# Issue queues by role, earlier X loads and later weight copies in the prologue of a spectral-filter and recurrent-attention kernel

## Chip, cores, metric

One core of one Trainium2 chip. The metric is the device time of one execution in microseconds (us); lower is better.

## The reference

Two independent computations share one launch, and their results are put side by side.

```python
# A: gated long convolution, q,k,v: (1, 2048, 1024)
kv  = k_shift(k, shift_k) * v               # 4-tap shift
y_f = rfft2(pad(kv)) * rfft2(pad(ssm_k))    # product in the frequency domain
y   = irfft2(y_f)[:2048] + kv * ssm_D
a   = q * y
# B: attention with a carried memory, x: (1, 2048, 1024), 32 heads of 128
for s in range(64):                         # 64 segments of 32 rows
    h = concat([mem, x[segment s]])         # mem: 8 rows
    qh, kh, vh = h @ Wq, h @ Wk, h @ Wv
    o = softmax(mask(qh @ kh.T * scale)) @ vh @ Wo
    mem = o[:8]                             # needed by the next segment
    b[segment s] = o[8:]
out = concat([a, b], axis=-1)
```

## The kernel before

The program has a prologue of about 460 us and a loop over the 64 segments of about 1736 us. The prologue computes A completely and, in between, those products of B that don't depend on the memory. It has these stages; I mark them by the instructions of TensorE (PE) and use these names throughout:

1. **Stage 1** (to the first matmul `kb_ps`): the first transform of A. The **first dense pass** follows (to the first `Kre_ps`): matmuls of B alone.
2. **Spectral stage** (to the last `z_ps`): 34 units, each of which gathers columns of two scratch tensors in HBM (`SK`, `SU`), multiplies in the frequency domain and stores to scratch `SZ`. After each unit `fill()` slips in a piece of B.
3. **Inverse stage** (to the last `y_ps`): 16 steps, each loads `zt` from `SZ` and `qt` from q, and writes one block of the output.
4. **Last dense pass** (to the first `vb_ps`), then the **V pass** (to the first `acc`, which is the start of the loop): x times Wv, stored to scratch `VBD`.

Each `nc.<engine>.dma_start` is an instruction in the in-order queue of that engine: while it waits for its source or its buffer, what is behind it in this queue isn't issued either. (In the profile before, SyncE's queue waits for an output's `ot` from 320.7 to 324.9 us; the `zt` load behind this output goes out right after it, at 325.3 us.) SyncE (SP in the profile) only issues; ScalarE (ACT) and GpSimd (POOL) compute and issue. The parts that matter, cut:

```python
# spectral stage
gather(Kt_, SK1, pr, nc.scalar)
gather(Ut, SU1, pr, nc.sync)
...
nc.gpsimd.tensor_tensor(out=Yre, in0=pa, in1=pb, op=ALU.subtract)
...
scatter(SZ, pr, zss[pi], nc.sync)           # waits for ScalarE's zs
# inverse stage
for t in range(16):
    (nc.sync if t % 2 == 0 else nc.gpsimd).dma_start(zt[:], SZ...[t])
    ...                                     # 4 matmuls into pt
    load_rows(qt, q, t, 0, nc.gpsimd if t % 2 == 0 else nc.sync)
    nc.vector.tensor_tensor(out=ot[:], in0=pt[:], in1=qt[:], op=ALU.mult)
    nc.sync.dma_start(rows_view(outa, t), ot[:])   # waits for VectorE's ot
    fill()
# pieces of B
def x_block(b):
    both = pair()                           # two buffers, taken in turn
    xq[b % 2].dma_start(both[:, 0:1024], x[...])   # xq = [nc.sync, nc.gpsimd]
    ...                                     # 8 transposes on PE, a copy on VectorE
    nc.gpsimd.dma_start(REC[...], xt)       # REC<-pair; frees the buffer
def fill():
    store()                                 # one waiting REC<-stage store, nc.gpsimd
    n = units[0]; units[0] += 1
    if n < 34 and n % 3 == 2 or n >= 34 and n % 3 == 0:
        if blocks: x_block(blocks.pop(0))
    if n >= 34 or n % 3 != 2:
        next(rest, None)                    # next head of a dense pass
# V pass
wv = [group(2, 0, temps), None]             # Wv loads on nc.sync
for _ in rest: store()                      # last dense pass
wv[1] = group(2, 1, temps)
place_late(4, stage_home); ...              # Wlate, Wmore loads, nc.gpsimd
for ch in ring_order:                       # copies HBM to HBM for the loop
    if ch[0] == 3:                          # the 6 streamed chunks of Wo
        nc.gpsimd.dma_start(dst_view(stream_src(ch), ch), dram_chunk(ch))
for g in range(2):
    for tb in range(4):
        vst = pair()...                     # the same two buffers
        for c in range(4):
            ...                             # 8 matmuls vb_ps, then evac to vst
        for c in range(4):
            nc.sync.dma_start(VBD[...], vst[:, c, :]...)
```

The Wo copies stand late in the source but wait for nothing, so the compiler's scheduler put them near the start of GpSimd's queue.

Of the kernel before, what the change touches and what calls it, by code (L numbers as in the profile page):

```python
# [31 lines left out]
def a_kernel(ctx: ExitStack, tc, q, k, v, shift_k, ssm_k, ssm_D, outa, slot4, slot16, stage1_done, fill):  # L32
    nc = tc.nc
# [18 lines left out]
    def rows_view(ap2d, t):  # L52
        return ap2d.rearrange("(p r) d -> r p d", r=16)[t]

    def load_rows(dst, src2d, t, lag, eng):
        c = t - lag
        if c >= 0:
            eng.dma_start(dst, rows_view(src2d, c))
        else:
            nc.gpsimd.memset(dst[0:1, :], 0.0)  # L60
            rv = rows_view(src2d, 16 + c)
            eng.dma_start(dst[1:113, :], rv[0:112])
            eng.dma_start(dst[113:128, :], rv[112:127])
# [205 lines left out]
    with ExitStack() as c2:  # L269
# [4 lines left out]
        def gather(dst, scratch, pr, eng):  # L274
            if pr <= 31:
                eng.dma_start(dst[:, :], scratch[4 * pr:4 * pr + 4].rearrange("m n d -> (m n) d"))
            else:
                eng.dma_start(dst[0:32, :], scratch[1])
                nc.gpsimd.memset(dst[32:64, :], 0.0)
                nc.gpsimd.memset(dst[64:128, :], 0.0)  # L280

        def scatter(scratch, pr, src, eng):
            if 1 <= pr <= 31:
                eng.dma_start(scratch[4 * pr:4 * pr + 4].rearrange("m n d -> (m n) d"), src[:, :])
            elif pr == 0:
                eng.dma_start(scratch[0], src[0:32, :])
                eng.dma_start(scratch[2:4].rearrange("m n d -> (m n) d"), src[64:128, :])
            else:
                eng.dma_start(scratch[1], src[0:32, :])

        def load_set(st):
            prs = [2 * st, 2 * st + 1] if st < 16 else [32]
            Us, Ks = [], []
            for pi, pr in enumerate(prs):
                Kt_ = gio.tile([128, 1024], BF, tag=f"Kg{pi}", name="Kg")
                gather(Kt_, SK1, pr, nc.scalar)
                Ut = gio.tile([128, 1024], BF, tag=f"Ug{pi}", name="Ug")
                gather(Ut, SU1, pr, nc.sync)
                Us.append(Ut)
                Ks.append(Kt_)  # L300
            return prs, Us, Ks
# [34 lines left out]
        def unit_back(st, prs, hf, Ys, zss):  # L336
            Yre, Yim = Ys
            for pi, pr in enumerate(prs):
                pt = ps1.tile([128, 512], F32, tag="p", name="z_ps")
                rs = slice(64 * pi, 64 * pi + 64)  # L340
                nc.tensor.matmul(pt[:, :], lhsT=Nre[rs, st, :], rhs=Yre[rs, :], start=True, stop=False,
                                 tile_position=(64 * pi, 0))
                nc.tensor.matmul(pt[:, :], lhsT=Nim[rs, st, :], rhs=Yim[rs, :], start=False, stop=True,
                                 tile_position=(64 * pi, 0))
                nc.scalar.copy(zss[pi][:, hf * 512:(hf + 1) * 512], pt[:])
            if hf == 1:
                for pi, pr in enumerate(prs):
                    scatter(SZ, pr, zss[pi], nc.sync)

        pending = None  # L350
        nxt = load_set(0)
# [13 lines left out]
    with ExitStack() as c3:  # L365
        io = c3.enter_context(tc.tile_pool(name="a3_io", bufs=4, side="right"))
        wk = c3.enter_context(tc.tile_pool(name="a3_wk", bufs=3, side="right"))
        ps_big = c3.enter_context(tc.tile_pool(name="a3_ps", bufs=3, space=PSUM))
        for t in range(16):
            pt = ps_big.tile([128, 1024], F32, tag="big", name="y_ps")  # L370
            zt = io.tile([128, 2, 1024], BF, tag="zt", name="zt")
            (nc.sync if t % 2 == 0 else nc.gpsimd).dma_start(zt[:], SZ.rearrange("m (h r) d -> r m h d", h=2)[t])
            for hf in range(2):
                for h in range(2):
                    nc.tensor.matmul(pt[:, hf * 512:(hf + 1) * 512], lhsT=G2h[h][:, :],
                                     rhs=zt[:, h, hf * 512:(hf + 1) * 512], start=(h == 0), stop=(h == 1))
            qt = io.tile([128, 1024], BF, tag="qt", name="qt")
            load_rows(qt, q, t, 0, nc.gpsimd if t % 2 == 0 else nc.sync)
            ot = wk.tile([128, 1024], BF, tag="ot", name="ot")
            nc.vector.tensor_tensor(out=ot[:], in0=pt[:], in1=qt[:], op=ALU.mult)  # L380
            nc.sync.dma_start(rows_view(outa, t), ot[:])
            fill()


def b_kernel(ctx: ExitStack, tc, x, mem0, Wq, Wk, Wv, Wo, outb, n_seg, run_a):
    nc = tc.nc
# [42 lines left out]
    def stream_src(ch):  # L429
        return WS[ring_order.index(ch), :, 0:2048]  # L430
# [87 lines left out]
    def make_xbt():  # L518
        xb = x.rearrange("(tb s t) d -> tb s t d", s=16, t=SEG)
        for tb in range(4):  # L520
# [5 lines left out]
            for h in range(2):  # L526
                nc.scalar.copy(XBT[h][:, :, 16 * tb:16 * tb + 16, :].rearrange("p k s t -> p k (s t)"),
                               tp[:, 512 * h:512 * h + 512].rearrange("p (k c) -> p k c", k=4))

    def group(m, g, temps={}, which=range(8), ws=None):  # L530
        ws = ws or [None] * 8
        for kc in which:
            ch = (m, kc, g)
            if ch in res:
                nc.sync.dma_start(res[ch], dram_chunk(ch))
                ws[kc] = res[ch]
            else:
                t = temps[ch]() if ch in temps else pw()
                nc.sync.dma_start(t[:], dram_chunk(ch))
                if ch in streamed:  # L540
                    nc.gpsimd.dma_start(stream_src(ch), t[:])
                ws[kc] = t[:]
        return ws

    def x_block(b):
        both = pair()
        X_sb = both[:, 0:1024]
        xq[b % 2].dma_start(X_sb, x[b * 128:(b + 1) * 128, :])
        tp = ps0.tile([128, 1024], BF, tag="ps0", name="xt_ps")
        for kc in range(8):  # L550
            nc.tensor.transpose(tp[:, kc * 128:(kc + 1) * 128], X_sb[:, kc * 128:(kc + 1) * 128], ident[:])
        xt = both[:, 1024:2048].rearrange("p (s k t) -> p s k t", s=4, k=8)
        nc.vector.tensor_copy(xt, tp[:].rearrange("p (k j t) -> p j k t", k=8, j=4))
        nc.gpsimd.dma_start(REC[:, 4 * b:4 * b + 4, 0:256], xt.rearrange("p s k t -> p s (k t)"))
# [51 lines left out]
    def fill():  # L606
        store()
        n = units[0]
        units[0] += 1
        if n < 34 and n % 3 == 2 or n >= 34 and n % 3 == 0:  # L610
            if blocks:
                x_block(blocks.pop(0))
        if n >= 34 or n % 3 != 2:
            next(rest, None)

    run_a(pw, slot16, stage1_done, fill)

# [42 lines left out]
    with c0p:  # L660
        temps = dict(zip(v_temp, homes_v))
        wv = [group(2, 0, temps), None]
        for _ in rest:
            store()
        wv[1] = group(2, 1, temps)
        while stores:
            store()
        place_late(4, stage_home)
        for i in range(len(v_temp) - 2, n_more):
            place_late(1, lambda: more(i))  # L670
        for _ in range(2):
            fetch()
        for ch in ring_order:
            if ch[0] == 3:
                nc.gpsimd.dma_start(dst_view(stream_src(ch), ch), dram_chunk(ch))
        for g in range(2):
            ws = wv[g]
            for tb in range(4):
                vst = pair()[:].rearrange("p (c w) -> p c w", c=4)
                for c in range(4):  # L680
                    ps = ps0.tile([128, 512], F32, tag="ps0", name="vb_ps")
                    for kc in range(8):
                        nc.tensor.matmul(ps[:], lhsT=xbt(kc)[:, 16 * tb:16 * tb + 16, :].rearrange("p s t -> p (s t)"),
                                         rhs=ws[kc][:, c * 512:(c + 1) * 512], start=(kc == 0), stop=(kc == 7))
                    evac(vst[:, c, :], ps[:])
                for c in range(4):
                    nc.sync.dma_start(
                        VBD[16 * tb:16 * tb + 16, :, c, :, g * 128:(g + 1) * 128].rearrange("s t i e -> (s t) i e"),
                        vst[:, c, :].rearrange("p (i e) -> p i e", i=4))
            if g == 0:  # L690
                place_late(4, stage_home)
                for i in range(2):
                    place_late(1, lambda: more(i))
        for i in range(2, len(v_temp) - 2):
            place_late(1, lambda: more(i))
        for k in (2, 3):
            if late:
                place_late(1, lambda: pw(k))
        assert not late
# [397 lines left out]
```

## Time and profile before

2196.51 us, median of 3 runs (2195.79 to 2200.39).

| what | number | view |
|---|---|---|
| loop, 64 segments | 1735.9 us, DMA share 1.00, 384 GB/s | windows |
| prologue | 459.7 us, of which the DMA engines idle some 50 to 60 us | windows |
| inverse stage | 74.9 us, DMA share 0.93 at 311 GB/s | windows |
| SyncE standing for `zs` and `ot` in the prologue | 42.3 and 40.2 us | waits |

The windows view of the kernel before: one row for each stage in the order above (the first dense pass is the second row, the loop the last). Columns as the second line says: busy us and number of instructions of each engine, granted TensorE clock, mean busy share of the 16 DMA engines, rate.

```profile
core 0: us, PE busy (x) PEld busy (x) DVE busy (x) ACT busy (x) POOL busy (x), PEclk, DMA share, GB/s
0.00:122.80 122.80, 69.02 (x297) 29.57 (x298) 101.17 (x205) 100.21 (x108) 33.77 (x55) 0.86 0.96 338
122.80:152.50 29.70, 29.70 (x130) 12.91 (x131) 3.46 (x5) 6.26 (x11) 0.00 (x0) 0.93 0.92 338
152.50:298.50 146.00, 125.92 (x683) 40.77 (x682) 109.20 (x189) 78.48 (x150) 66.61 (x68) 0.93 0.81 272
298.50:373.40 74.90, 49.46 (x212) 21.11 (x212) 24.62 (x25) 5.81 (x10) 22.48 (x32) 0.84 0.93 311
373.40:390.80 17.40, 17.40 (x82) 7.90 (x81) 4.47 (x9) 3.52 (x6) 1.81 (x3) 1.00 1.01 375
390.80:459.70 68.90, 59.48 (x264) 25.79 (x266) 8.14 (x14) 12.80 (x22) 17.23 (x28) 0.95 0.82 254
459.70:2195.60 1735.90, 1388.46 (x33981) 792.02 (x33981) 622.92 (x2240) 441.25 (x833) 302.51 (x955) 0.99 1.00 384
```

Stage 1 has a full DMA system (share 0.96), and VectorE and ScalarE are each busy for 82% of it. In the spectral stage PE is busy for 125.9 of 146.0 us. The loop is limited by its weight stream; the chain of waits of the whole span says the same (engines, then the largest entry by line):

```profile
DMA 15%; PE 6%; DVE 2%; issue 1%; ACT 0%; POOL 0%; DVEq 0%; POOLq 0%; SPq 0%; ACTq 0%
```

Its largest entry by line is the ring of streamed weights, also 15%. So only the prologue can move. The waits of SyncE's queue there (total us, times, longest us):

```profile
SPq L284 <- ACT zs L345: 42.3, 12, 7.0
SPq L381 <- DVE ot L380: 40.2, 14, 7.7
```

L284 is a store to `SZ`, L381 a store of an output block. While one of these stands, the gathers or the `zt` and `qt` loads behind it stand too. In the V pass, ScalarE and VectorE wait for the two staging buffers, which a `VBD` store frees when it lands:

```profile
ACT pair L561 <- DMA VBD<-pair: 9.2, 2, 6.1
DVE pair L563 <- DMA VBD<-pair: 6.4, 1, 6.4
```

And the timeline of GpSimd shows where the six Wo copies are issued (start us, us, instruction):

```profile
33.75 0.68 POOL L675 DMA_DIRECT2D WS<-in_B_Wo_dram  x1
...
40.63 2.06 POOL L675 DMA_DIRECT2D WS<-in_B_Wo_dram  x3
...
48.13 1.39 POOL L675 DMA_DIRECT2D WS<-in_B_Wo_dram  x2
```

### The profile page before, as it was taken

What the parts mean: (1) busy time and instruction counts of PE and PEld (TensorE: products, weight loads), DVE (VectorE), ACT (ScalarE), POOL (GpSimd) and SP (SyncE); (2) the same over time, 40 slices, a digit from 0 to 9 for tenths busy, and PEclk for the clock granted to TensorE, in tenths of its full rate; (3) what the DMA queues carried; (4) which work ended last, traced back from release to release, by engine and by line L of the source; (5) the groups of instructions that cost most, each with busy time, mean ns of one, the idle gap of its engine ahead of it and who ended that gap; (6) DMA issues with size and microseconds to landing.
All of it is one profiled execution on the core that took longest, in us unless ns stands there. A gap on an engine that the chain in (4) does not pass through costs nothing. (4 is left out here: it accounts for less than half of the span.)

```text
span 2195.6 us, 81532 instructions
## 1 busy us (share of the span) xinstructions
PE 1739.5 (79%) x35636; PEld 930.1 (42%) x35636; DVE 874.0 (40%) x2686; ACT 648.3 (30%) x1139; POOL 444.4 (20%) x1139
## 2 busy tenths in 40 slices
PE   4687886878778878788888887887878787888886
PEld 2232233334444444444444444444544444444444
DVE  8836752123333333333333333333333333333333
ACT  7845530122222222222222222222222222222222
POOL 5013432201112111111111111111112211111111
PEclk9888998999999999999999999999999999999999
DMA  9998869979999999999999999999999999999997
GB/s 336 338 346 297 279 230 331 336 262 395 373 380 388 382 383 391 389 386 384 390 392 395 392 394 390 392 396 386 390 383 386 389 383 383 392 392 383 386 389 270
DMA packets 261678, 804.66 MB, mean 366 GB/s; under 512 B 52332, under 2 KB 52364, under 8 KB 261319
## 3 DMA queue, kind: packets, MB, share of 16 engines
q1 hardware_dynamic: 227816, 721.58, 86.2%
q0 software_dynamic: 28272, 67.31, 9.2%
q10 hardware_dynamic: 5232, 10.55, 1.5%
q8 instruction: 279, 4.57, 0.9%
q14 instruction: 79, 0.65, 0.1%
HBM read 739.92 MB, written 62.39 MB: 365 GB/s over the span
## 5 line engine op out<-in xcount | busy, mean ns | idle before, releaser
L873 PEld LDWEIGHTS <-rec 128*32 128x32 bf16 x12351 | 322.4, 96 | 470.9 <-issue 252.0
L873 PE MATMUL acc<-wring,rec 128*32 128x512 bf16 (+1 forms) x3777 | 375.6, 385 | 137.0 <-DMA wring<-WS 123.7
L882 ACT CAST qkv_sb<-acc 128x512 bf16<-128x512 f32 x384 | 225.1, 586 | 657.1 <-PE acc L873 657.1
L959 PEld LDWEIGHTS <-OT 128*32 128x32 bf16 x8192 | 218.7, 97 | 181.0 <-issue 153.2
L959 PE MATMUL yacc<-wring,OT 128*32 128x256 bf16 x3072 | 154.7, 277 | 100.7 <-DMA wring<-WS 58.5
L873 PE MATMUL acc<-Wmid,rec 128*32 128x512 bf16 x3072 | 226.6, 385 | 0.0
L873 PE MATMUL acc<-Wres,rec 128*32 128x512 bf16 x2816 | 222.3, 382 | 0.0
L819 PEld LDWEIGHTS <-OTB 128*16 128x16 bf16 x4096 | 104.9, 90 | 102.8 <-issue 92.6
L945 ACT CAST OT<-OTp 128x512 bf16<-128x512 f32 x128 | 75.1, 586 | 242.1 <-PE OTp L937 242.1
L975 DVE COPY KT<-tps 128x512 bf16<-128x512 bf16 x64 | 27.2, 425 | 298.7 <-PE tps L888 298.7
L774 POOL DMA_DIRECT2D rec<-REC x64 | 37.5, 585 | 519.4 <-issue 282.7
L946 DVE CAST OTB<-OTp 128x128 bf16<-128x128 f32 x128 | 37.4, 292 | 260.4 <-ACT OT L945 260.4
L725 DVE TENSOR_SCALAR wring<-OTp 128x384 int32<-128x384 int32 x126 | 112.3, 891 | 59.3 <-PE acc L873 49.0
L873 PE MATMUL acc<-pw,rec 128*32 128x512 bf16 x1536 | 130.3, 382 | 0.0
L849 POOL COPY KT<-rec 128x128 bf16<-128x128 bf16 x128 | 38.8, 303 | 426.8 <-PE SB L897 422.7
L834 POOL DMA_DIRECT2D out_dram<-YB x128 | 73.3, 579 | 238.5 <-DVE YB L832 225.3
L903 DVE TENSOR_REDUCE mx<-SB 128x5 f32<-128x200 f32 x128 | 47.1, 368 | 175.8 <-PE SB L897 175.8
L819 PE MATMUL SB<-wring,OTB 128*16 128x256 bf16 x1488 | 78.8, 275 | 39.7 <-DVE SB L798 32.6
L888 PE MATMUL tps<-ident,qkv_sb 128*128 128x128 bf16 x1024 | 101.0, 221 | 8.2 <-DVE wring L725 0.2
L888 PEld LDWEIGHTS <-qkv_sb 128*128 128x128 bf16 x1024 | 62.7, 97 | 105.6 <-ACT qkv_sb L882 65.4
L1015 ACT CAST Y<-yacc 128x256 bf16<-128x256 f32 x64 | 23.8, 373 | 248.0 <-PE yacc L959 244.1
L959 PE MATMUL yacc<-Wlate,OT 128*32 128x256 bf16 x2048 | 94.4, 276 | 2.2 <-issue 2.1
(231 smaller groups left out, 2706.3 us busy)
## 6 DMA issues: line engine op xcount, KB each, us to landing
wring<-WS SPq DMA_DIRECT2D x1216, 512.0 KB, 7.4
rec<-REC POOLq DMA_DIRECT2D x64, 192.0 KB, 6.1
SK<-s_sb SPq DMA_DIRECT2D x16, 512.0 KB, 5.9
SU<-s_sb SPq DMA_DIRECT2D x16, 512.0 KB, 4.9
Kg<-SK ACTq DMA_DIRECT2D x32, 256.0 KB, 4.8
Ug<-SU SPq DMA_DIRECT2D x32, 256.0 KB, 5.3
REC<-stage POOLq DMA_DIRECT2D x16, 512.0 KB, 9.0
SZ<-zs SPq DMA_DIRECT2D x31, 256.0 KB, 5.2
```

The source lines that it names most:

```text
L725: nc.vector.tensor_scalar(out=dst, in0=src, scalar1=0, scalar2=None, op0=ALU.bitwise_or)
L774: nc.gpsimd.dma_start(rec[:], REC[:, s, :])
L819: nc.tensor.matmul(self.acc[32 * dq:32 * dq + W, x - o:y - o], lhsT=self.OTB[:, c, 4 * g + i, :], rhs=r, start=first and not self.seeded, ...
L834: nc.gpsimd.dma_start(bass.AP(outb.tensor, outb.offset + (SEG * NB * self.b + NX) * 2048 + 256 * dq, [[2048 * SEG, NB], [2048, 8], [1, 256 ...
L849: nc.gpsimd.tensor_copy(KT[:, :, :, 32:40], KBs[:, 128 * g:128 * g + 128].rearrange("p (c i t) -> p i c t", c=4, i=4))
L873: nc.tensor.matmul(self.acc[32 * c:32 * c + 32, x - 512 * c:y - 512 * c], lhsT=hT[:, kc, :], rhs=r, start=(kc == 0 and x == 512 * c), stop ...
L882: nc.scalar.copy(sb[:], self.acc[:])
L888: nc.tensor.transpose(tp[:, i * 128:(i + 1) * 128], sb[:, i * 128:(i + 1) * 128], ident[:])
L903: nc.vector.tensor_reduce(out=mx[:], in_=S, op=ALU.max, axis=AX.X)
L945: nc.scalar.copy(OT[:], o_view[:, :, :, 0:32])
L946: nc.vector.tensor_copy(OTB[:, :, 4 * g:4 * g + 4, 8 * j:8 * j + 8], o_view[:, :, :, 32:40])
L959: nc.tensor.matmul(yacc[32 * dq:32 * dq + 32, x - o:y - o], lhsT=OT[:, c, i, :], rhs=r, start=(h == 0 and x == o), stop=(h == 31), tile_po ...
```

## The change

The intent: every queue has one role in the prologue, so that no load stands behind a store that waits for an engine; the X blocks are loaded two units before they are used; and bytes that nobody needs early (six Wo copies of 512 KB, and some late weight loads) leave the full stage 1 and go to the V pass, which has spare transfer time. `tc.issue_after(ins)` tells the scheduler to place the instructions inside it behind `ins` in their engine's order.

```diff
-                gather(Kt_, SK1, pr, nc.scalar)
+                gather(Kt_, SK1, pr, nc.sync)
@@ unit_back
-                    scatter(SZ, pr, zss[pi], nc.sync)
+                    scatter(SZ, pr, zss[pi], nc.scalar)
@@ inverse stage
-            (nc.sync if t % 2 == 0 else nc.gpsimd).dma_start(zt[:], SZ...[t])
+            nc.sync.dma_start(zt[:], SZ...[t])
-            load_rows(qt, q, t, 0, nc.gpsimd if t % 2 == 0 else nc.sync)
+            load_rows(qt, q, t, 0, nc.sync)
-            nc.sync.dma_start(rows_view(outa, t), ot[:])
+            nc.gpsimd.dma_start(rows_view(outa, t), ot[:])
@@ group
-                    nc.gpsimd.dma_start(stream_src(ch), t[:])
+                    copied.append(nc.gpsimd.dma_start(stream_src(ch), t[:]))
@@ X blocks
+    loaded = []
+    def x_load(b):
+        both = pair()
+        nc.sync.dma_start(both[:, 0:1024], x[b * 128:(b + 1) * 128, :])
+        loaded.append(both)
     def x_block(b):
-        both = pair()
+        both = loaded.pop(0)
         X_sb = both[:, 0:1024]
-        xq[b % 2].dma_start(X_sb, x[b * 128:(b + 1) * 128, :])
@@ fill
-        if n < 34 and n % 3 == 2 or n >= 34 and n % 3 == 0:
-            if blocks:
-                x_block(blocks.pop(0))
+        if n % 3 == 2 and blocks:
+            x_block(blocks.pop(0))
         if n >= 34 or n % 3 != 2:
             next(rest, None)
+        if n % 3 == 0 and len(blocks) > len(loaded):
+            x_load(n_seg // 4 - len(blocks))
@@ V pass
-        place_late(4, stage_home)
-        for i in range(len(v_temp) - 2, n_more):
-            place_late(1, lambda: more(i))
+        with tc.issue_after(copied[-4].ins):
+            place_late(4, stage_home)
+            for i in range(len(v_temp) - 2, n_more):
+                place_late(1, lambda: more(i))
         for _ in range(2):
             fetch()
-        for ch in ring_order:
-            if ch[0] == 3:
-                nc.gpsimd.dma_start(dst_view(stream_src(ch), ch), dram_chunk(ch))
+        with tc.issue_after(copied[-1].ins):
+            for ch in ring_order:
+                if ch[0] == 3:
+                    nc.gpsimd.dma_start(dst_view(stream_src(ch), ch), dram_chunk(ch))
```

More of the change, by code (lines that the diff above doesn't have):

```diff
@@ L371, in a_kernel @@
             zt = io.tile([128, 2, 1024], BF, tag="zt", name="zt")
-            (nc.sync if t % 2 == 0 else nc.gpsimd).dma_start(zt[:], SZ.rearrange("m (h r) d -> r m h d", h=2)[t])
+            nc.sync.dma_start(zt[:], SZ.rearrange("m (h r) d -> r m h d", h=2)[t])
             for hf in range(2):
@@ L528, in make_xbt @@
                                tp[:, 512 * h:512 * h + 512].rearrange("p (k c) -> p k c", k=4))
+    copied = []
     def group(m, g, temps={}, which=range(8), ws=None):
```

## The prediction

> What bounds the kernel now. Span 2195.6 us. The timeline shows the recurrent loop of 64 segments starting at 458 us; the windows view then gives DMA share 1.00 to 1.03 and 380 to 400 GB/s. The loop, 1737 us, is limited by streamed weights (chain of waits: DMA wring<-WS 15%, its largest entry). The change leaves it alone; only the 458 us prologue can move.
>
> Prologue by windows: stage 1 (0 to 122 us) has DMA 0.95 and VectorE about 0.88, two limits at once. The spectral stage with the first dense passes (152 to 300 us) has PE at 9.2 to 10 of 10 us in its good stretches, one unit each 3.6 us (34 units would be 123 us; they took 147), and three gaps. The inverse stage (303 to 373 us) has DMA 0.93 to 1.01. The V pass (390 to 458 us) first waits for Wv, then is PE bound; DMA is 0.36 to 0.45 from 440 to 460 us. In sum the DMA engines idle about 50 us in the prologue; re-ordering can win no more.
>
> What changes, costed.
> 1. K gathers move from ScalarE to SyncE, SZ stores from SyncE to ScalarE: as many issues as before (33 and 34, 0.33 to 0.45 us each), but less blocking. SyncE waited 42 us for ScalarE's zs (12 waits), gathers standing behind; ScalarE stood 5.6 us at 175 us and 8.7 us at 261 us around a Kg gather.
> 2. X blocks are loaded two units earlier, all on SyncE. The waits view has PE waiting 21.8 us in 4 waits for pair<-x (5.6 us at 185, 7.2 at 345, 3.1 at 366, the rest earlier).
> 3. Outputs go to GpSimd: SyncE's 40 us of waits for ot no longer stand before zt and qt loads. DMA is full there, so ordering alone wins little: the Trainium skill, "DMA: Bandwidth & Descriptors", section "Issuing engines are not separate DMA queues", says all issuers share the same 16 DMA engines; the full DMA share agrees.
> 4. Six Wo copies (3.1 MB, 9.4 us each to landing) move from 34 to 49 us, and four Wlate loads and one Wmore load (2.6 MB) from 366 to 376 us, into the V pass. At 390 GB/s that is an estimated 8 and 7 us of DMA time, taken from full stretches and put where some 12 us are idle. PE stands about 6 us at 391 to 399 us for Wv behind those loads.
>
> On the critical path, estimated: spectral stage -8 us (half of the gaps; the one at 177 to 190 us lies in a stretch of DMA 1.0 and stays in part), inverse stage and start of the V pass -9 us, stage 1 -4 us (VectorE and ScalarE nearly full, so part of 8 us), V pass and loop start +1 us for the copies. Sum -20 us.
>
> Predicted: 2176 us, 8 in 10 between 2154 and 2192. Faster by over 2% (below 2152.6 us): 0.08; within 2%: 0.91; slower: 0.01.
>
> What would show it: loop start near 438 us, loop still 1737 us; SyncE's waits for zs and ot gone; PE waits for pair<-x below 8 us; ScalarE's two gaps gone; DMA share above 0.8 at the end of the V pass; Wv landing before the last dense pass ends.
>
> What would make it wrong: all loads on SyncE block each other (a gather waiting for a buffer holds X and Wq loads); GpSimd, holding outputs that wait for VectorE, delays the REC stores and so the X buffers; the copies reach into the loop start; or the scheduler's static order turns out different. If transfers alone bind, the gain is under 10 us; if all gaps close, it nears 40 us.

## The result and the profile after

2189.35 us, median of 4 runs (2186.19 to 2192.14), against 2196.61 us of the kernel before. The ratio is 0.9963, 95% interval 0.9944 to 0.9983. Ratios here and below are the mean time of one kernel's fast runs over that of the other's of the same rounds, so not quite the ratio of the medians quoted. The change gains about 8 us where 20 were predicted. The run after_again below gave 0.9995 (0.9969 to 1.0021), so even the 8 us are near what repeats can tell.

Two notes on reading the numbers. First, the loop, which no edit touches, took 1728.6 to 1742.9 us in the 20 profiled executions, a spread of 14 us: the total can't resolve a few us, so I judge by the stages of the prologue, in which marks of the same program agree within about 5 us (from one pair, after and after_again). Second, the prologue's stages slide into each other (a dense matmul that the inverse stage doesn't fit in comes later), so the sum from the last `z_ps` to the loop start is safer than one stage.

The windows of the kernel after, by the same marks:

```profile
0.00:115.60 115.60, 65.78 (x296) 28.66 (x297) 100.78 (x205) 99.93 (x108) 28.99 (x48) 0.89 0.96 332
115.60:145.40 29.80, 29.80 (x130) 12.90 (x131) 3.46 (x5) 6.29 (x11) 0.00 (x0) 0.93 0.86 319
145.40:292.40 147.00, 126.36 (x687) 41.52 (x686) 109.08 (x190) 79.22 (x150) 62.68 (x61) 0.94 0.80 273
292.40:352.40 60.00, 48.09 (x210) 19.91 (x210) 24.12 (x25) 5.85 (x10) 17.39 (x26) 0.89 0.99 369
352.40:369.40 17.00, 17.00 (x80) 7.74 (x79) 4.34 (x9) 3.51 (x6) 4.03 (x8) 1.00 1.01 368
369.40:454.00 84.60, 59.72 (x260) 26.07 (x258) 8.13 (x14) 12.78 (x22) 22.38 (x35) 0.88 0.81 262
454.00:2190.40 1736.40, 1387.89 (x33981) 790.73 (x33981) 622.09 (x2240) 440.81 (x833) 301.37 (x955) 0.99 1.00 384
```

The loop is unchanged (1735.9 and 1736.4 us). Stage 1 lost 7.2 us, the spectral stage nothing (+1.0), the inverse stage 14.9, and the V pass grew by 15.7: what the inverse stage won, the V pass gave back. The rate of the inverse stage went from 311 to 369 GB/s while its DMA share only went from 0.93 to 0.99. The chain of waits is still the loop's:

```profile
DMA 14%; PE 5%; DVE 2%; issue 1%; ACT 0%; POOL 0%; SPq 0%; DVEq 0%; POOLq 0%; ACTq 0%
```

The waits for `ot` between 290 and 380 us: SyncE's are nearly gone, because the outputs (L381) wait on GpSimd's queue, where no `zt` or `qt` load stands behind them. (L58 is the `qt` load.)

```profile
SPq L58 <- DVE ot L380: 7.9, 9, 2.1
```

and of GpSimd:

```profile
POOL out_dram L381 <- DVE ot L380: 33.1, 15, 4.9
```

The waits of ScalarE and VectorE for the two staging buffers of the V pass, which a `VBD` store frees when it lands, have grown from 9.2 and 6.4 us to:

```profile
ACT pair L569 <- DMA VBD<-pair: 27.9, 2, 16.4
DVE pair L571 <- DMA VBD<-pair: 18.0, 1, 18.0
```

And here is why those stores land late. GpSimd's timeline from 390 us on: thirteen transfers of 512 KB come in one burst of 16 us (6.8 MB; at the loop's 384 GB/s they alone would need an estimated 18 us). Nine of them are moved ones: the six Wo copies, two Wlate loads and the Wmore load. (The other two of the four tied Wlate loads still went out at 367 us, as before.) The last four, Wlate loads from Wo, belonged to the V pass before too, and went out as far into it (31 us; here 33 to 38). The median landing of a Wo copy here is 12.8 us, and the slowest `VBD` store took 21.1 us to land, against 15.9 before.

```profile
392.48 1.08 POOL L658 DMA_DIRECT2D Wlate<-in_B_Wk_dram  x2
393.55 0.72 POOL L658 DMA_DIRECT2D Wmore<-in_B_Wo_dram  x1
394.25 2.74 POOL L686 DMA_DIRECT2D WS<-in_B_Wo_dram  x4
...
400.70 0.65 POOL L686 DMA_DIRECT2D WS<-in_B_Wo_dram  x1 [0.80 <-DMA Wlate<-in_B_Wk_dram]
402.42 0.74 POOL L658 DMA_DIRECT2D Wlate<-in_B_Wo_dram  x1 [1.06 <-DMA Wlate<-in_B_Wk_dram]
...
407.10 0.72 POOL L658 DMA_DIRECT2D Wlate<-in_B_Wo_dram  x1 [1.07 <-DMA WS<-in_B_Wo_dram]
```

The burst falls where the DMA engines counted as busy in the kernel before too (share 0.95 or more up to 440 us). Their idle time lies at the end of the V pass, and there it stayed: a share of 0.40 in the last 19.7 us before, 0.42 in the last 20 us after. Two stretches of the V pass after:

```profile
390.00:410.00 20.00, 8.49 (x32) 3.44 (x32) 0.69 (x1) 1.66 (x3) 10.41 (x15) 0.83 1.04 330
...
434.00:454.00 20.00, 19.02 (x90) 8.59 (x88) 3.29 (x7) 4.46 (x8) 3.36 (x8) 1.00 0.42 83
```

PE stands behind ScalarE, which stands behind the store (two lines of PE's timeline; in brackets the idle time before the instruction and what ended it):

```profile
396.73 0.59 PE L694 MATMUL vb_ps<-Wres,XBT 128*128 128x512 bf16 x1 [7.61 <-ACT pair L569]
...
419.43 0.59 PE L694 MATMUL vb_ps<-Wres,XBT 128*128 128x512 bf16 x1 [14.20 <-ACT pair L569]
```

### The profile page after: what moved, and what is told of

Its sections match the earlier page's. It is cut to its first block, busy times and chain, and to the rows that moved or that the text cites. A ratio compares the mean times of both kernels' runs of the same rounds, so it can differ in the third digit from the quotient of the medians.

```text
span 2190.4 us, 81498 instructions
## 1 busy us (share of the span) xinstructions
PE 1734.6 (79%) x35636; PEld 927.5 (42%) x35636; DVE 872.0 (40%) x2686; ACT 648.4 (30%) x1139; POOL 436.8 (20%) x1131
## 5 line engine op out<-in xcount | busy, mean ns | idle before, releaser
L970 PE MATMUL yacc<-wring,OT 128*32 128x256 bf16 x3072 | 153.9, 275 | 98.0 <-DMA wring<-WS 56.4
L956 ACT CAST OT<-OTp 128x512 bf16<-128x512 f32 x128 | 74.9, 585 | 242.9 <-PE OTp L948 242.9
L736 DVE TENSOR_SCALAR wring<-OTp 128x384 int32<-128x384 int32 x126 | 112.2, 890 | 58.4 <-PE acc L884 52.4
```

The costliest lines, as they stand in the source:

```text
L736: nc.vector.tensor_scalar(out=dst, in0=src, scalar1=0, scalar2=None, op0=ALU.bitwise_or)
L956: nc.scalar.copy(OT[:], o_view[:, :, :, 0:32])
L970: nc.tensor.matmul(yacc[32 * dq:32 * dq + 32, x - o:y - o], lhsT=OT[:, c, i, :], rhs=r, start=(h == 0 and x == o), stop=(h == 31), tile_po ...
```

## The experiments

The theories that the runs were to part:

- **Copies**: moving the Wo copies takes bytes out of stage 1, but in the V pass they delay the `VBD` stores. *Rivals*: the tie of the Wlate loads does it; or the bytes themselves cost it, not their coming in a burst.
- **Inverse stage**: the loads no longer stand behind outputs. *Rivals*: only one half of the swap matters (loads on SyncE, or outputs on GpSimd); or the swap of gathers and stores in the spectral stage does it.
- **Spectral stage**: its gaps are bytes in front of an X block, so neither queues nor an earlier issue close them. *Rival*: the two staging buffers or the issue order.

All 18 runs gave the right result. The table has the stages of each profiled execution, in us, in the order in which the kernels are told. "Tail" is the sum of inverse stage, last dense pass and V pass. "Loop at" is where the loop starts. The ratio is to the kernel before.

| run | stage 1 | spectral | inverse | V pass | tail | loop at | ratio (95%) |
|---|---|---|---|---|---|---|---|
| before | 122.8 | 146.0 | 74.9 | 68.9 | 161.2 | 459.7 | 1 |
| after | 115.6 | 147.0 | 60.0 | 84.6 | 161.6 | 454.0 | 0.9963 (0.9944–0.9983) |
| after_again | 117.5 | 148.5 | 59.5 | 79.4 | 156.0 | 449.8 | 0.9995 (0.9969–1.0021) |
| wo_free | 121.6 | 147.2 | 60.0 | 73.8 | 150.8 | 449.0 | 0.9964 (0.9937–0.9992) |
| wo_spread | 113.8 | 148.0 | 63.3 | 76.5 | 156.8 | 448.0 | 0.9958 (0.9932–0.9984) |
| copies_only | 115.8 | 144.9 | 71.2 | 84.4 | 173.1 | 461.5 | 1.0040 (1.0016–1.0064) |
| queues_only | 122.3 | 148.1 | 56.8 | 59.4 | 145.8 | 443.9 | 0.9961 (0.9931–0.9991) |
| queues_x | 121.3 | 147.3 | 59.9 | 75.4 | 152.4 | 451.4 | 0.9986 (0.9959–1.0013) |
| x_only | 121.8 | 141.3 | 77.8 | 74.8 | 164.0 | 454.8 | 1.0013 (0.9985–1.0041) |
| queues_spread | 116.2 | 148.8 | 60.5 | 63.3 | 152.0 | 446.8 | 0.9955 (0.9930–0.9980) |
| loads_sp | 121.9 | 145.4 | 80.7 | 67.3 | 165.3 | 460.3 | 0.9987 (0.9949–1.0024) |
| out_pool | 123.3 | 145.7 | 76.1 | 69.9 | 163.5 | 462.1 | 1.0021 (0.9971–1.0072) |
| inverse_only | 122.3 | 144.9 | 57.6 | 56.9 | 145.7 | 442.3 | 0.9950 (0.9918–0.9982) |
| gs_only | 122.9 | 148.2 | 72.9 | 67.1 | 157.5 | 458.4 | 1.0002 (0.9965–1.0039) |
| stores_slow | 122.7 | 147.8 | 58.7 | 75.0 | 151.2 | 451.3 | 0.9959 (0.9914–1.0005) |
| wo_paced | 115.5 | 148.9 | 59.5 | 75.0 | 151.6 | 443.7 | 0.9933 (0.9898–0.9968) |
| queues_paced | 118.1 | 153.9 | 58.4 | 65.9 | 149.8 | 451.2 | 0.9956 (0.9925–0.9988) |
| stores_late | 122.2 | 143.6 | 57.7 | 63.6 | 147.4 | 442.4 | 0.9914 (0.9886–0.9943) |
| after_paced_late | 115.8 | 135.7 | 59.4 | 75.1 | 151.6 | 430.9 | 0.9924 (0.9907–0.9940) |
| inverse_late | 121.1 | 137.5 | 57.3 | 56.8 | 145.5 | 433.1 | 0.9946 (0.9928–0.9963) |

### after_again: the change, unaltered

No edit; it runs beside the parts of the change, to show the spread.

> The changed kernel unchanged, as a measure of how far stage times of one program differ from run to run: first loop matmul at 454 us and fourth segment at 568.9 us, each within 2 us; V pass 84.6 us within 2 us.

2193.74 us against 2192.71, ratio 0.9995. In the profiled execution the V pass took 79.4 us, and the loop started at 449.8. So the V pass is longer than before by 10.5 to 15.7 us in two executions, and the loop starts 5.7 to 9.9 us sooner. Differences of under some 5 us in one stage are not told apart here.

### wo_free: the copies back where they were

Edit, on the kernel after:

```diff
-        with tc.issue_after(copied[-1].ins):
-            for ch in ring_order:
-                if ch[0] == 3: ...
+        for ch in ring_order:
+            if ch[0] == 3: ...
```

> The changed kernel, but the six Wo copies are not tied behind the last V copy, so they are issued in stage 1 again. Theory 1 (the burst of 13 transfers of 512 KB on the GpSimd queue at 392 to 408 us, of which the six copies are nearly half, holds up the VBD stores, so the two staging buffers of the V pass come free late): V pass falls from 81 to about 70 us, stage 1 grows from 116 to about 121 us, in all 2184 us, 5 us under the changed kernel. Theory 2 (the prologue is set by its bytes, wherever they are issued): V pass stays above 78 us, in all 2189 to 2193 us.

2185.61 us against 2191.79. Stage 1 is back at 121.6 us and the V pass shrinks to 73.8: the copies' move is worth −4 to −6 us in the one and +6 to +11 in the other. The wait of ScalarE for `VBD<-pair` falls from 27.9 to 16.1 us: of its two waits the first, which begins before the burst, hardly changes (11.5 and 10.7 us), the second falls from 16.4 to 5.4. The move of the copies, the third part of the change, gains nothing net.

### copies_only: the kernel before with the moved copies alone

Edit, on the kernel before: the list `copied` and both `issue_after`, nothing else of the change.

> The kernel before with only the copies moved behind the V copies (queues and X loads as before). Theory 1: stage 1 ends at about 116 us as in the changed kernel, V pass at 75 us or more, in all within 4 us of before (2193 to 2199 us). Theory 2: within 3 us of before as well, but with the V pass no longer than 70 us. If moving the copies was what gained, 2189 us.

2202.61 us against 2191.79, and its interval, 1.0016 to 1.0064, excludes no change: alone, the move loses (more than the expected 4 us). Stage 1 −7.0 us, V pass +15.5, tail +11.9. ScalarE's wait for `VBD<-pair` is 28.8 us. Both this pair and the one above show the same trade, so it doesn't depend on the queues.

### wo_spread and queues_spread: the copies in the spectral stage

Edit, on the kernel after, and (queues_spread) on queues_only, in place of the loop of Wo copies; `MARK[0]` is the unit's subtraction on GpSimd:

```diff
+        if 28 <= n < 34 and wo:               # in fill()
+            ch = wo.pop(0)
+            with tc.issue_after(MARK[0].ins):
+                nc.gpsimd.dma_start(dst_view(stream_src(ch), ch), dram_chunk(ch))
```

> The changed kernel with the six Wo copies issued one per unit in units 28 to 33 of the spectral stage, where its DMA share is 0.21 to 0.27. Theory 1: stage 1 stays at 116 us, spectral stage within 2 us, V pass 81 to about 70 us, in all about 2179 us. Theory 2: DMA share rises there but the end does not move, 2187 to 2191 us.

> Queue roles alone, with the six Wo copies issued one per unit in units 28 to 33 of the spectral stage. Theory 1 (the copies cost nothing where DMA has room): stage 1 ends at 115 us, the fourth segment at 553 to 555 us (queues alone: 560.3), in all about 0.3% faster than the queues alone. Theory 2 (bytes decide): fourth segment at 559 to 562 us.

Half a miss. Stage 1 kept its gain (113.8 and 116.2 us) and the spectral stage didn't lengthen, but the tail grew by 6.0 us (wo_spread against wo_free) and 6.2 us (queues_spread against queues_only): copies issued at the end of the spectral stage probably push the transfers of the inverse stage, whose DMA share is 0.99, but 6 us is about the spread. The times, 2184.70 and 2184.73 us, are those of the kernels without the copies' move.

### wo_paced: the same bytes in the V pass, one copy at a time

This parts the burst from the bytes. Edit, on the kernel after: the loop of Wo copies is taken out; in the V pass, behind the four `VBD` stores of a block:

```diff
-                    nc.sync.dma_start(
+                    last_vbd = nc.sync.dma_start(
                         VBD[...], vst[:, c, :]...)
+                if wo and (g, tb) >= (0, 1):
+                    ch = wo.pop(0)
+                    with tc.issue_after(last_vbd.ins):
+                        nc.sync.dma_start(dst_view(stream_src(ch), ch), dram_chunk(ch))
```

> The changed kernel with the six Wo copies issued on SyncE, one behind the VBD stores of each of six of the eight row blocks of the V pass, so the same bytes in the same pass without the burst. Theory 1 (burst): stage 1 115 to 118 us, V pass 72 to 75 us (changed kernel 84.6 and 79.4, untied copies 73.8), first loop matmul at 443 to 446 us. Theory 2 (bytes): V pass 79 us or more, loop from 450 us on.

2182.09 us against 2195.49, ratio 0.9933. Windows of its stage 1 and its V pass:

```profile
0.00:115.50 115.50, 64.86 (x297) 28.95 (x298) 100.81 (x205) 99.65 (x108) 28.74 (x48) 0.84 0.96 332
...
368.70:443.70 75.00, 61.83 (x260) 26.64 (x258) 8.13 (x14) 12.79 (x22) 18.38 (x29) 0.89 0.93 293
```

The V pass moves as many bytes as after (22.0 MB and 22.2 MB: 75.0 us × 293 GB/s, 84.6 us × 262 GB/s), but takes 75.0 us, and stage 1 keeps its gain. The waits for the staging buffers fall, and a Wo copy lands in 5.3 us (median) instead of 12.8:

```profile
ACT pair L569 <- DMA VBD<-pair: 16.7, 2, 10.7
```

So it isn't the bytes that cost, but when they come: with the copies paced, the tail is 151.6 us, as long as that of wo_free (150.8), which doesn't have them there at all. The edit changes three things at once: the copies are apart, most come later (397.7 to 436.5 us, so that the DMA share at the end of the V pass rises to 0.70), and SyncE issues them in place of GpSimd. Which of these counts is not parted. In the timed ratios the repair isn't clear of noise: 0.9933 (0.9898 to 0.9968) against 0.9963 (0.9944 to 0.9983) for the change.

### queues_paced: the paced copies on the queues alone

Edit: as wo_paced, on queues_only.

> Queue roles alone, with the Wo copies paced behind the VBD stores of the V pass. Theory 1 (burst): stage 1 115 to 118 us, last dense pass and V pass together no longer than the 89 us of the queues alone, first loop matmul at 437 to 441 us (queues alone 443.9), the fourth segment ends at 553 to 557 us. If the V pass has no room: first loop matmul at 444 us or later.

A miss: the loop starts at 451.2 us. Stage 1 is 118.1 (queues_only 122.3), but the spectral stage took 153.9 us, although PE's order of instructions up to there is the same as in queues_only; the lower granted clock may account for some of it (0.90 over 153.9 us is an estimated 15 us of full clock lost; 0.93 over 148.1 us in queues_only is 10). The tail is 149.8 us, 4.0 more than queues_only. One profiled execution can't tell a chance from a cost here, and the timed ratio, 0.9956, is that of queues_only.

### queues_only, queues_x and x_only: the other two parts, alone and together

Edits: queues_only is the kernel before with the first five changed lines of the diff. x_only is the kernel before with `x_load`, `x_block` and `fill` of the kernel after. queues_x is the kernel after without both `issue_after`.

> The kernel before with only the queues of gathers, SZ stores, inverse-stage loads and outputs changed. Theory 1: stage 1 ends at 122 us, the inverse stage is shorter by about 8 us, V pass about 68 us, in all about 2188 us. If the queues bring nothing and the early X loads do: 2195 to 2198 us.

> The changed kernel with none of the copies and late loads tied: queue roles and early X loads alone. Theory 3 (the early X loads, all on SyncE, make gathers and weight loads wait behind X loads that wait for a buffer, and so cost time): first loop matmul at 447 to 451 us, like the 449.0 us of the run with only the Wo copies untied, and the fourth segment ends at about 562 us, a little after the 560.3 us of the queues alone. Rival: the tie of the Wlate loads is what costs, and this run begins the loop at 441 to 444 us, fourth segment at 558 to 560 us.

> The kernel before with only the early X loads, all on SyncE. Theory 3: no gain, the fourth segment ends at 573 to 580 us (before: 574.6), in all 0 to 4 us slower than before. If early X loads are worth what the prediction gave them: fourth segment at about 569 us.

2185.81 us (of 2191.79), 2192.19 (of 2192.71), 2196.64 (of 2192.71). The queues alone have the whole gain of the change: loop start 15.8 us earlier, tail 145.8. The earlier X blocks show no gain in time: alone 1.0013, and with the queues the loop starts 7.5 us later than without, which is more than the usual spread, but the timed intervals overlap. With X early the last dense pass is shorter (17.1 us instead of 29.6; in queues_only PE waits 4.4 us for an X block in it), but the V pass, which then starts sooner, is longer by 16.0; ScalarE waits 17.9 us for `VBD<-pair` in it (5.2 in queues_only), so that wait doesn't need the copies. In the spectral stage the early X loads do something in x_only alone: PE's waits for X blocks fall from 11.6 to 6.5 us and the stage takes 141.3 us, 4.7 less than before, about the spread. With the queues changed too they do nothing (queues_x 147.3 us and 13.4 us of waits, queues_only 148.1 and 11.9). Whether X loads and K gathers on one queue hold each other up, as the prediction feared, no run parts. The rival for the V pass, the tie of the Wlate loads, has no support: queues_x is without it and starts its loop at 451.4 us, wo_free has it and starts at 449.0.

### loads_sp, out_pool, inverse_only and gs_only: which swap of queues matters

Edits, each on the kernel before:

```diff
 loads_sp:      zt and qt loads all on nc.sync
 out_pool:      output stores on nc.gpsimd
 inverse_only:  both of these
 gs_only:       K gathers on nc.sync, SZ stores on nc.scalar
```

> The kernel before with only the loads of the inverse stage all on SyncE (outputs stay on SyncE). Theory 4 (half of these loads on the GpSimd queue is what holds the stage at 333 GB/s with the DMA engines counted busy): inverse stage 60 us at about 385 GB/s. Rival (outputs that wait for VectorE on SyncE stand before the loads, so too few transfers are in flight): inverse stage 72 us or more, as before.

> The kernel before with only the outputs of the inverse stage moved to GpSimd (loads alternate between SyncE and GpSimd as before). Theory 4: inverse stage stays at 70 us or more and below 350 GB/s. Rival (blocking of SyncE by outputs): inverse stage 60 to 64 us at about 385 GB/s.

> The kernel before with both halves of the inverse stage's change (loads on SyncE, outputs on GpSimd), gathers and SZ stores as before. If the two together are the gain (each alone left 76 to 81 us): inverse stage 57 to 62 us at about 385 GB/s, first loop matmul at 444 to 450 us. If the gathers and SZ stores matter for it: 68 us or more.

> The kernel before with only K gathers on SyncE and SZ stores on ScalarE. The prediction gave this and the X loads 8 us in the spectral stage. From the stage table so far: spectral stage 145 to 149 us, no gain; inverse stage 72 to 78 us; in all within 4 us of before.

Neither half of the inverse stage's swap does anything alone (80.7 and 76.1 us, before 74.9; so each theory missed once, theory 4 in loads_sp and its rival in out_pool); together they take 17.3 us off it (57.6), and the loop starts 17.4 us earlier. This is far outside the spread: the 14 rows of the table with both halves have 56.8 to 63.3 us in this stage, the 6 without 71.2 to 80.7. inverse_only took 2184.42 us against 2197.00, ratio 0.9950. gs_only is 2199.75 us, ratio 1.0002, spectral stage 148.2: the swap in the spectral stage is worth nothing. The windows of the inverse stage of loads_sp, out_pool and inverse_only, one each:

```profile
295.00:375.70 80.70, 47.76 (x212) 20.09 (x212) 24.59 (x25) 5.80 (x10) 13.34 (x19) 0.79 0.90 298
```

```profile
298.60:374.70 76.10, 49.25 (x211) 20.57 (x211) 24.63 (x25) 5.81 (x10) 28.93 (x44) 0.80 0.86 303
```

```profile
296.60:354.20 57.60, 44.39 (x196) 18.65 (x195) 22.78 (x23) 5.80 (x10) 16.98 (x25) 0.88 1.00 372
```

Their waits for `ot` in the queues, from 290 to 380 us, show the reason. loads_sp: the outputs stay on SyncE, now in front of all loads.

```profile
SPq L381 <- DVE ot L380: 47.6, 16, 7.6
```

out_pool: the outputs wait on GpSimd, where every second `zt` and `qt` load still is.

```profile
POOL out_dram L381 <- DVE ot L380: 32.5, 11, 8.0
```

In inverse_only the outputs wait as long (30.4 us), but no `zt` or `qt` load stands behind them. SyncE's queue:

```profile
SPq L58 <- DVE ot L380: 6.8, 6, 2.5
```

and of GpSimd:

```profile
POOL out_dram L381 <- DVE ot L380: 30.4, 14, 5.2
```

In this stage the waits cost where loads stood behind them, and didn't where none did; with either half alone there was still such a queue. It is no general law: the gathers behind the waits for `zs` cost nothing (gs_only).

### stores_slow and stores_late: the gaps of the spectral stage

In the kernel after, PE waits for an X block at about 174 to 180 us (in queues_only at 178 to 185), while the DMA share is 1.04: four stores `REC<-stage` of 512 KB, those of the first dense pass, are handed out one a unit from the stage's start on. Edits, on queues_only:

```diff
 stores_slow:
-        store()
+        if n % 3 == 1:
+            store()
 stores_late:
-        store()
+        if n >= 12:
+            with tc.issue_after(MARK[0].ins):
+                store()
```

> Queue roles alone, with the REC stores of the dense passes issued one per three units and not one per unit. If the two gaps of the spectral stage (at about 174 and 260 us) come from stretches in which weight loads, ring copies and REC stores fill the DMA engines before the gathers and X loads: spectral stage 148 to about 141 us, PE's waits for pair<-x in it below 6 us (12.7 us in the changed kernel). If they come from the order of the queues: no change, 146 to 150 us.

> Queue roles alone, with the four REC stores (2.1 MB) of the first dense pass held back by the issue order until unit 12 of the spectral stage. If the gap at 174 to 185 us is made by the bytes in front of it: it closes by an estimated 5 us (2.1 MB at 390 GB/s), spectral stage 141 to 144 us. If it is the order of SyncE's queue (gathers and X loads behind weight loads that wait): no change, 146 to 150 us.

stores_slow tells nothing: the spectral stage is 147.8 us, but all four early stores were still issued by 173 us, since nothing tied them to their unit. stores_late ties them: 2177.63 us against 2197.00, ratio 0.9914. Its spectral stage is 143.6 us, and the wait for the X block at the gap is gone; a gap of 3.3 us, in which PE waits for ScalarE's `Kre`, remains at 181 to 184 us. Windows of 30 us, from 10 us after the start of the stage: first queues_only, then stores_late.

```profile
160.00:190.00 30.00, 18.97 (x100) 6.00 (x98) 14.25 (x24) 10.60 (x21) 10.41 (x11) 0.83 0.93 351
```

```profile
161.40:191.40 30.00, 25.40 (x133) 8.02 (x132) 20.44 (x37) 15.50 (x30) 10.34 (x11) 0.89 0.94 348
```

PE is busy 25.4 us of 30 in place of 19.0 at the same DMA share, and its wait for X in the stage falls from 11.9 to 1.8 us (queues_only, then stores_late):

```profile
PE xt_ps L551 <- DMA pair<-in_B_x_dram: 11.9, 2, 7.5
```

```profile
PE xt_ps L552 <- DMA pair<-in_B_x_dram: 1.8, 1, 1.8
```

Holding the stores back also changed the static order of PE's instructions (of the first 3000 matmuls, 421 work on another tile than the one in the same place in queues_only), so how much of it is the bytes and how much the order is open.

### after_paced_late and inverse_late: the parts that helped, together

Edits: wo_paced with the edit of stores_late; inverse_only with the edit of stores_late.

> The changed kernel with the Wo copies paced through the V pass and the REC stores of the first dense pass held until unit 12. If the two repairs add up: stage 1 about 116 us, spectral stage 143 to 145 us, V pass about 75 us, first loop matmul at 437 to 441 us, in all 0.8 to 1.2% faster than before. If they don't: first loop matmul at 443 us or later.

> The kernel before with only the inverse stage's queues and the REC stores held until unit 12: no early X loads, no moved copies, gathers and SZ stores as before. If these two are all that the case has to give: spectral stage 140 to 143 us, inverse stage 57 to 60 us, first loop matmul at 437 to 441 us, as fast as the run above. If the gathers and SZ stores had a part in what the late stores won: spectral stage 145 us or more.

2172.15 us against 2188.79, ratio 0.9924; 2178.78 us against 2188.79, ratio 0.9946. after_paced_late has the lowest time of all, and its whole interval, 0.9907 to 0.9940, lies below that of the change, 0.9944 to 0.9983. It is the version that I would keep, though stores_late (0.9914, of fewer rounds) and wo_paced (0.9933) can't be told from it. Its spectral stage, with 123.42 us of work on PE:

```profile
143.60:279.30 135.70, 123.42 (x676) 41.02 (x686) 106.87 (x190) 78.85 (x150) 62.48 (x61) 0.96 0.90 300
```

The three runs with held stores took 143.6, 137.5 and 135.7 us there, mean 138.9; the other seventeen rows of the table lie from 141.3 to 153.9, mean 147.2. Two cautions. The two shortest are below what was expected, and had a higher granted clock in this stage (0.96 and 0.98; 0.94 in stores_late); an estimated 3 to 6 us of their lead over stores_late may be clock. They were run at other times. And the timed ratios show no clear gain of the held stores: stores_late 0.9914 beside queues_only 0.9961, inverse_late 0.9946 beside inverse_only 0.9950, after_paced_late 0.9924 beside wo_paced 0.9933, with overlapping intervals each time. The loop of after_paced_late starts 28.8 us earlier than in the profiled execution of the kernel before; the timed gain is about 17 us. Most of the other 12 us are between calls: that profiled execution took 2197.4 us, while in the last call the kernel before had a median of 2188.79.

## Why the prediction was wrong in size

The prediction's sum against the two profiled executions of the changed kernel, each minus the kernel before:

| term | predicted | measured |
|---|---|---|
| stage 1 | −4 | −7.2 and −5.3 |
| spectral stage | −8 | +1.0 and +2.5 |
| inverse stage and start of the V pass | −9 | inverse stage alone −14.9 and −15.4 |
| V pass and loop start, for the copies | +1 | V pass +15.7 and +10.5 |
| loop start in sum | −20 | −5.7 and −9.9 |
| loop | 0 | +0.5 and −3.8 |

**Right.** The loop is the limit of the kernel and didn't change. Stage 1 gains from the copies leaving it: the twelve rows of the table with the copies in it have a mean of 122.2 us, the eight without them 116.0. SyncE's waits for `zs` went away, and those for `ot` fell from 40.2 to 7.9 us. Three of its own signs failed: the loop starts at 454 us (438 foretold), PE waits 13.8 us for X blocks (below 8), and the DMA share at the end of the V pass is 0.42 (above 0.8).

**The V-pass term failed most: "V pass and loop start +1 us for the copies".** I had priced the moved 5.7 MB at about 15 us of DMA time and set it against 12 idle us. (Two of the loads, 1 MB, didn't move in the end.) The bytes do fit: wo_paced moves as many there for 151.6 us of tail, where wo_free has 150.8 without the copies. What I had wrong is the overlap with the idle time, which lies at the end of the pass: the Wo copies went out at 394 to 401 us, where the DMA share was 1.04. And I left out what stands behind them while they are in flight. They came at once, the `VBD` stores landed late, two staging buffers were too few to cover it, and PE stood. The prediction did name "the copies reach into the loop start" as a risk, but not this wait in the middle. Of the growth, 6 to 11 us are the Wo copies (the V pass of wo_free against two executions of the changed kernel). A part remains that goes with X early (V pass 59.4 us in queues_only, 75.4 in queues_x), most of it matched by a shorter last dense pass; its cause stays open.

**"Spectral stage -8 us" didn't come.** It rested on the swap of gathers and `SZ` stores and on the earlier X loads. gs_only (148.2 us) shows that the first is worth nothing: SyncE's 42 us of waits for `zs` were off the critical path. The second didn't reach the gaps: with X early PE still waits 12.7 us for X blocks there (11.6 before), probably because the loads are issued into a full DMA system behind the `REC` stores and, with two staging buffers, SyncE's X loads wait 30.7 us in 8 waits of the prologue for one to come free. In x_only, where K gathers aren't on SyncE, they wait 22.6 us and the stage is 4.7 us shorter, so the new queue may have a part in it. Holding 2.1 MB of stores back shortened the stage in three profiled executions (138.9 us against 147.2), though no timed ratio confirms it. The prediction had said of one gap that it "lies in a stretch of DMA 1.0 and stays in part"; it stayed nearly whole (PE's gaps in it are 5.1 and 5.6 us before, 3.1 and 6.6 after).

**"DMA is full there, so ordering alone wins little" was false**, to the prediction's fortune. I took the DMA share of 0.93 in the inverse stage for a full system. The stage moved 23.3 MB in 74.9 us before and 22.1 MB in 60.0 us after: 311 and 369 GB/s, or 334 and 373 while busy (rate over share). For the same reason "re-ordering can win no more" than the idle time was no bound. Why the engines count as busy while they move less is not shown. The Trainium skill, "Perfetto Trace Analysis", section "Identifying the Most-Contended Engine", says that for DMA one should use HBM utilization in place of occupancy, as 16 engines make occupancy misleading. This agrees, with 311 and 369 GB/s at shares of 0.93 and 0.99; the rate stood beside the share in the windows I had read.

So the mechanism of the queues was right for the inverse stage and undersized, the copies' price was undersized by a factor of 6 to 11 (6 to 11 us where the prediction had +1; with X early the V pass grew by 10 to 16), and the spectral gain was not there. That the inverse stage won 15 us against 9 for it and the V pass start together is luck: it covered part of the other two misses.

## What to carry to other kernels

Price a wait in an issue queue by what stands behind it and whether that is needed at once: parting loads and waiting stores won nothing for the 42 us of waits for `zs`, and 15 to 17 us for the 40 us of waits for `ot`, but only once they were parted on both queues. When transfers are moved into a stretch with idle DMA time, see where in the stretch the idle time lies, and meter them out behind that stretch's own stores: the same bytes cost 5 to 11 us of the tail in a burst ahead of the idle time, and within the spread nothing when paced. And read the rate beside the busy share before calling a stretch full.

## What the Trainium skill lacked or had wrong

- "DMA: Bandwidth & Descriptors", section "Issuing engines are not separate DMA queues", says that issuing from several engines saves only the sequencer's time for starting a DMA. The section lacks the in-order queue: a load behind an output that waits for its data can't start. (The page's section on the GpSimd path does have the issuing sequencer make this wait, but not what that costs the loads behind.) Parting them took the inverse stage from 74.9 to 57.6 us (23.3 and 21.4 MB). The prediction leaned on this sentence and undersized the gain.
- "Perfetto Trace Analysis", section "DMA Optimizations", advises one engine for inputs and another for outputs, above all in loops. The case agrees (inverse_only, ratio 0.9950). It lacks that half of the separation is worth nothing: 80.7 and 76.1 us against 74.9 before.
- "DMA: Bandwidth & Descriptors", section "Anatomy of one DMA — SWDGE (gpsimd) path", fits the time of one DMA issued from GpSimd as about 2.0 us plus bytes over 436 GB/s, which for 512 KB is an estimated 3.2 us. Under load the traces show a median landing of 7.2 us for weight loads of this size issued from GpSimd in the V pass before, and 12.8 us for the Wo copies in the burst (those go from HBM to HBM). The fit has no term for other transfers in flight, which is what a schedule needs.
